# Another written-out order for the last attention chunk and the folds, with the folds' adds all on VectorE

## The chip, the cores and the metric

The kernel runs on one NeuronCore of a Trainium2 chip (trn2). The metric is device time in microseconds (us); a time of the kernel is the median over runs. The engines are called PE (TensorE), DVE (VectorE), ACT (ScalarE), POOL (GpSimd) and SP (SyncE, which issues the loads and stores). PEld is PE's weight load.

## The reference

The inputs are q, k, v (2 batches, 8 heads, 768 tokens, 64 features), a decay per head, and the weights of two MLPs (512 to 2048 to 512). The reference runs retention in blocks, then a 2-D Fourier transform's real part with an MLP, then a second MLP:

```python
for b in range(nb):                      # retention
    intra = einsum('bhic,bhjc->bhij', qb, kb) * Dmask
    intra = einsum('bhij,bhjd->bhid', intra, vb)
    inter = einsum('bhid,bhde->bhie', qb * lam_pow, kv_state)
    out[:, :, sl] = intra + inter
    kv_state = lam_block * kv_state + einsum('bhsd,bhse->bhde', kb * rev_pow, vb)
X = fft(fft(x, axis=1), axis=2)          # x: [2, 768, 512]
u = x + real(X)
u = u + relu(layernorm(u) @ w_ch1) @ w_ch2
return u + relu(layernorm(u) * g_ln @ w2_ch1) @ w2_ch2
```

## The kernel before

**Tiling.** The 768 tokens of a batch are six chunks of 128. Retention goes chunk by chunk. Chunks 3 to 5 are laid in mirrored order into the upper half of the tile U, so that the first transform (along the tokens) can fold token t with token 768 - t; row 0 of each mirrored tile has to be moved to its neighbour, which ACT does with copies of one row. Each fold gives an even half (cosine) and an odd half (sine), and each half is folded once more along the features. Five groups of matmuls for each of three folds then make the first transform, a second transform follows, then a layer norm and the first MLP. Values that must keep more than 16 bits are held as a high and a low float16 half; ACT makes the high half (a cast), POOL or DVE the low one (a subtraction). Weights arrive as 64-bit numbers in DRAM and are put together from bit fields: ACT takes the upper part (top), DVE shifts the lower part, DVE joins both (or), then come the two halves.

**What sets the order.** Up to the last chunk of the first batch, and again behind the layer norm of its first half, a planner lays the instructions out by simulated time and by priorities. Between these two, the order on PE, DVE, POOL and ACT is written out by hand in the string ORDER (line 44). Each word of it advances one chain by one step (line 957 on), and each engine works through its own instructions in that order. The words are:

- S: the score matmuls of chunk 5 (PE). B1, B0: the masked scores of the two heads' halves: DVE multiply with the mask (L353), ACT high half (L356), POOL low half (L358).
- s: the state behind chunk 4: POOL decay (L451), PE matmuls (L458), DVE add (L465), two ACT copies (L470).
- O4, O5: the outputs of chunks 4 and 5: 24 PE matmuls (L426), DVE sum into u (L432), ACT row copies. The matmuls need both halves of the masked scores.
- I: chunk 5's part from the state: PE matmuls (L375), DVE scaling into int (L379). O5's sum needs it.
- k0 to k2, j0 to j2: the cosine and the sine half of fold 0, 1, 2 (fold_half): an add or subtraction of two tiles in SBUF (L489), a half-fold (L491), two quarters (L494 and L495, or L497 and L498). The add runs on POOL if the fold's name, e0 to e2 for k and o0 to o2 for j, is in the string ONPOOL (line 50), otherwise on DVE.
- R: the fold of row 0 alone: four POOL instructions (L408 to L411), an ACT cast (L414), a POOL low half (L416).
- c0 to c3: the conversion of the first four weight chunks (conv_steps).
- d24, d20, ...: the first transform's matmuls of fold 2 for group 4, and so on. Those of fold 0 close a group; d04, d01 and d00 are followed by two matmuls with the row's halves. D0 to D4: ACT copies of the groups' results.
- q, X, p, P: the second transform, with a subtraction on DVE and, for X1 and X2, one on POOL. b, n: the layer norm; its power (L650) is on POOL. W: warm-up matmuls on PE whose results nobody reads, so many as the number says. M: the first MLP's first matmuls.

**Buffers near the change.** The score matmuls use two of three PSUM banks called "at"; d24 and d23 use that pool next. A weight chunk's joined value lies in one of three buffers (wtp), so c3 uses that of c0. The row fold and fold 0's odd half use the same place in SBUF, one after the other.

Of the kernel before, what the change touches and what calls it, by code (L numbers as in the profile page):

```python
# [20 lines left out]
B, H, S, D = 2, 8, 768, 64  # L21
# [20 lines left out]
YS = 2.0 ** -15  # L42

ORDER = """
c0 S B1 s O4 B0 O4 B0 O4 B1 s s c0 R k2 j2 s k2 c0 B0 I B1 c0 I k2 O5 O5 j2 c1 O5 j2 W12 d24 O5 d20 j1 k1 c3
k1 k0 k1 j1 d21 d22 k0 j1 d23 j0 j0 k0 j0 W6 d10 c2 d11 d14 R d13 d12 d03 c3 d02 D3 R c2 c1 c3 D2 d04 d01 D4
d00 D1 q0 D0 q0 c3 q2 q2 X0 X0 q1 q1 X1 p0 p1 P0 c1 X1 P1 b0 b1 b0 X2 c2 p2 b0 b1 X2 c1 P2 c2 b0 n0 b1 b2 b1
W27 n0 b2 n1 n0 b2 W6 n1 n0 b2 M00 n2 n1 n2 n2 n1 M01 M12 M11 M10 n2 M22 M20 M02 M21
"""
ONPOOL = "Y1 Y2 o0 o1 k0 k1 k2 j0 j1 j2"  # L50
LD1 = ()
LD2 = ()
EARLY0, GATEN, B1, SPC, DS, DC, DFO, DD, D1S, D2S, AO, YA, NR, NE, LN1, L1, L2, F01, F02, TL, R1, R2, SE, PR1, LAG, UB, FB, NW, MQ, SPL = 11, 8, 3, 2.0, 2.0, 5, 1.0, 0.5, 0.5, 1.0, "aba", "aa", 2, 0, 2, 2.5, 2.5, 16, 4, 3, 1.5, 2, "dddd_dppp", 0, 3, 3, 13, 11, 1, 3
# [71 lines left out]
def tile_retention_fourier_mlp(ctx: ExitStack, tc: tile.TileContext, a: dict, out: bass.AP):  # L125
# [20 lines left out]
    def bank(which, name):  # L146
        return banks[which].tile([P, 512], F32, tag=which, name=name)
# [103 lines left out]
    def w_load(kind, m, i, room=None):  # L251
        t = room
        if t is None:
            t = wst.tile([P, 512, 2], I32, tag="ws", name=f"ws{kind}_{m}_{i}")
        staged[kind, m, i] = t
        return sp.dma_start(t.rearrange("p n two -> p (n two)").bitcast(I16)[:, :2047], w_src(kind, m, i).bitcast(I16)[:, 1:2048])
# [11 lines left out]
    def w_conv(kind, m, i):  # L268
        return run(conv_steps(kind, m, i, "at"))
# [13 lines left out]
    def conv_steps(kind, m, i, which=None, into=None):  # L283
        if (kind, m, i) not in staged:
            w_load(kind, m, i)
        raw = staged.pop((kind, m, i))
        top = tops[n_top[0] % 3]
        n_top[0] += 1
        t = wtp.tile([P, 512], F32, tag="wt", name=f"wf{kind}_{m}_{i}")
        ti = t.bitcast(I32)  # L290
        part = ti if which is None else bank(which, f"ps_w{kind}_{m}_{i}").bitcast(I32)
        act.activation(top[:, :, 1], raw.bitcast(BF16)[:, :, 2], AF.Copy, scale=TOPS)  # L292
        dve.tensor_scalar(part, raw[:, :, 0], 13, None, op0=ALU.logical_shift_right)  # L293
        yield t
        dve.tensor_tensor(ti, part, top.rearrange("p n two -> p (n two)").bitcast(I32), op=ALU.bitwise_or)  # L295
        yield t
        if kind == 1:
            g, k = divmod(i, 4)
            if (m, g) not in w1t:
                w1t[m, g] = wpool.tile([P, 2, 4, 512], F16, tag=f"w1_{g}", name=f"w1_{m}_{g}")  # L300
            hi, lo = w1t[m, g][:, 0, k], w1t[m, g][:, 1, k]
        else:
            if into is None:
                into = w2t[m, i] = wpool.tile([P, 2, 512], F16, tag=f"w2_{i}", name=f"w2_{m}_{i}")
            hi, lo = into[:, 0], into[:, 1]
        if kind == 1 and m == 1:
            act.activation(t, t, AF.Copy, scale=gcol[:, k:k + 1])  # L307
        act.copy(hi, t)  # L308
        yield t
        (dve if m == 0 and i in (LD1 if kind == 1 else LD2) else pool).tensor_tensor(lo, t, hi, op=ALU.subtract)  # L310
        yield t
# [57 lines left out]
    def attn_i_steps(b, c, bk):  # L369
        t = f32t(f"int{b}_{c}")  # L370
        lp_ = lp[:, 1 if c >= 3 else 0]
        if b == 0:
            ps = bank(bk["i"], f"ps_i{b}_{c}")
            for i in range(H // 2):
                pe.matmul(ps[:, i * P:(i + 1) * P], loaded["qt", b, c][:, i * P:(i + 1) * P], diag[(c - 1) % 2][:, i],  # L375
                          start=True, stop=True)
            yield
            to, ti = (z.rearrange("p (h d) -> p h d", h=H) for z in (t, ps))
            dve.tensor_tensor(to, ti, lp_.unsqueeze(2).to_broadcast([P, H, D]), op=ALU.mult)  # L379
            xt[b, c] = t  # L380
            yield
            return
        both = [bank(bk["i"], f"ps_i{b}_{c}_{e}") for e in range(2)]
        with tc.manual_schedule(engines={mybir.EngineType.PE}):
            for i in range(H // 2):
                for e, ps in enumerate(both):
                    cols, r = slice(i * D, (i + 1) * D), slice(e * D, (e + 1) * D)
                    pe.matmul(ps[:, cols], loaded["qt", b, c][r, i * P:(i + 1) * P], states[(c - 1) % 2][r, cols],
                              start=True, stop=True)
        yield  # L390
        for e, ps in enumerate(both):
            to = t.rearrange("p (i e d) -> p i e d", e=2, d=D)[:, :, e]
            ti = ps[:, :H // 2 * D].rearrange("p (i d) -> p i d", d=D)
            dve.tensor_tensor(to, ti, lp_[:, e::2].unsqueeze(2).to_broadcast([P, H // 2, D]), op=ALU.mult)
        xt[b, c] = t
        yield
# [23 lines left out]
    def attn_o_steps(b, c, bk):  # L420
        ps = bank(bk["o"], f"ps_o{b}_{c}")
        for h in range(H):
            (i, e), hc = divmod(h, 2), slice(h * D, (h + 1) * D)
            m_, mc = ms[b, c, e], slice(i * P, (i + 1) * P)
            for n, (x, y) in enumerate(PASS):
                pe.matmul(ps[:, hc], m_[:, x, mc], vs[b, c][:, y, hc], start=n == 0, stop=n == 2)  # L426
        yield
        x_ = U[b][c] if c < 3 else U[b][8 - c]
        if c == 0:
            dve.tensor_scalar(x_, ps, XS, None, op0=ALU.mult)  # L430
        else:
            dve.scalar_tensor_tensor(x_, ps, XS, xt[b, c], op0=ALU.mult, op1=ALU.add)  # L432
        yield
        if c == 3:
            row0[b] = f32t(f"row0{b}", 4 if b == 0 else None)
            act.copy(row0[b][0:1], x_[0:1])
            if b > 0:
                run(row_fold(b))
        elif c > 3:
            act.copy(U[b][9 - c][0:1], x_[0:1])  # L440
        yield
        if c == NCH - 1:
            act.copy(x_[0:1], row0[b][0:1])
        yield

    def attn_s_steps(b, c, bk):
        new, old = states[c % 2], states[(c - 1) % 2]
        if c > 0:
            dec = stp.tile([P, H // 2 * D], F32, tag="dec", name=f"dec{b}_{c}")
            do, di = (z.rearrange("p (i d) -> p i d", d=D) for z in (dec, old))  # L450
            pool.tensor_tensor(do, di, lc.unsqueeze(2).to_broadcast([P, H // 2, D]), op=ALU.mult)  # L451
        yield
        k_ = ks[b, c]
        ps = bank(bk["st"], f"ps_st{b}_{c}")
        for h in range(H):
            (i, e), hc = divmod(h, 2), slice(h * D, (h + 1) * D)
            for n, (x, y) in enumerate(PASS):
                pe.matmul(ps[e * D:(e + 1) * D, i * D:(i + 1) * D], k_[:, x, hc], vs[b, c][:, y, hc],  # L458
                          start=n == 0, stop=n == 2)
        yield  # L460
        psv = ps[:, :H // 2 * D]
        if c == 0:
            dve.tensor_copy(new, psv)
        else:
            dve.tensor_tensor(new, psv, dec, op=ALU.add)  # L465
        yield
        if b == 0:
            for e in range(2):
                r = slice(e * D, (e + 1) * D)
                act.copy(diag[c % 2][r, :, e * D:(e + 1) * D], new[r].rearrange("p (i d) -> p i d", d=D))  # L470
        yield
# [456 lines left out]
    def eng(n):  # L928
        return pool if n in ONPOOL.split() else dve

    wide = {}
    chains = {"s": lambda: attn_s_steps(0, 4, bk0), "O4": lambda: attn_o_steps(0, 4, bk0),
              "O5": lambda: attn_o_steps(0, 5, bk0), "I": lambda: attn_i_steps(0, 5, bk0), "R": lambda: row_fold(0)}
# [5 lines left out]
    for g in range(5):  # L939
        chains[f"D{g}"] = lambda g=g: dft1_out(0, g, ps1[g])  # L940
    for i in range(NE, 4):
        chains[f"c{i}"] = lambda i=i: conv_steps(1, 0, i)
    for j in range(3):
        chains[f"q{j}"] = lambda j=j: dft2_q(0, j, bk0)
        chains[f"X{j}"] = lambda j=j: sub_sin(0, j, eng(f"Y{j}"))
# [59 lines left out]
    for c in range(NCH):  # L1005
        t = B1 + SPC * c
# [29 lines left out]
    n0 = (NB - 1) * NF  # L1036
# [16 lines left out]
    def step(n):  # L1053
        m = n // (NB * NF)
        return m, order[m][n // NF % NB], n % NF
# [3 lines left out]
    for (m, blk), f in fast_from.items():  # L1059
        for kk in range(2):  # L1060
            if m == 0 and blk < 3:
                put(16 * blk + f / 2 + kk - 3, lambda blk=blk, kk=kk: un_sums(0, blk, kk))
            else:
                at = m * NB * NF + order[m].index(blk) * NF
# [4 lines left out]
    for n in range(total + LAG):  # L1069
        rest = None  # L1070
        if n < total:
            m, blk, f = step(n)
# [34 lines left out]
```

## Time and profile before

| | |
|---|---|
| time, median of 3 runs | 611.54 us (611.45 to 612.33) |
| profiled execution | 611.77 us, its span 610.0 us |
| PE busy | 580.4 us, 95% of the span |
| DVE busy | 416.1 us, 68% |
| POOL busy | 285.9 us, 47% |
| ACT busy | 263.4 us, 43% |
| DMA | 63.23 MB, mean 104 GB/s |

The profile is of one execution. A busy share is an average over the whole span; the stages differ. The page also cuts the span into 40 slices of 15.25 us and gives the busy tenths of each engine; PE's begin with 6 8 6 9 9 and go on with 9 nearly everywhere. The written-out order covers about 32 to 75 us. The granted clock of PE is a share of full speed: 1.00 is the 2.4 GHz level, 0.50 the 1.2 GHz level.

### The profile page before, as it was taken

How to read it: one execution, taken by the hardware profiler on the slowest of the kernel's cores; microseconds unless marked ns; L12 is line 12 of the kernel's file. 1: busy time of each engine (PE TensorE's matmuls, PEld its weight loads, DVE VectorE, ACT ScalarE, POOL GpSimd, SP SyncE). 2: the span in 40 equal slices, each digit the busy share in tenths (PEclk: the TensorE clock that was granted, in tenths of full speed). 3: DMA queues.
4: the chain of work that ended last, by engine and by line, in shares of the span. 5: the costliest groups of instructions: out<-in, count | busy, mean ns of one | idle time of the engine just before them, and what ended most of it. 6: DMA issues, size and time to landing. Idle time of an engine off the chain costs nothing.

```text
span 610.0 us, 11891 instructions
## 1 busy us (share of the span) xinstructions
PE 580.4 (95%) x4675; PEld 381.4 (63%) x4675; DVE 416.1 (68%) x903; ACT 263.4 (43%) x530; POOL 285.9 (47%) x296
## 2 busy tenths in 40 slices
PE   6869989999999999899997999999999999999997
PEld 3754845566554555576765776666677677777773
DVE  5995699876596589886697778877444653445333
ACT  3644489764232433443456665853222222221120
POOL 7864879995443585451348765963021200020000
PEclk8878999999999999999998999999999999999999
DMA  8994149973000010353153542510111025102001
GB/s 278 396 401 135 44 133 268 337 243 122 2 1 0 19 35 2 81 144 121 45 163 119 177 158 99 162 33 1 53 27 27 2 74 66 18 1 81 24 1 52
DMA packets 46326, 63.23 MB, mean 104 GB/s; under 512 B 26176, under 2 KB 28350, under 8 KB 46270
## 3 DMA queue, kind: packets, MB, share of 16 engines
q1 hardware_dynamic: 45598, 62.40, 33.3%
q8 instruction: 36, 0.59, 0.4%
q10 hardware_dynamic: 672, 0.08, 0.1%
q14 instruction: 20, 0.16, 0.1%
HBM read 52.23 MB, written 6.29 MB: 96 GB/s over the span
## 4 chain that ended last, share of the span: by engine, by line
PE 59%; DVE 21%; ACT 8%; POOL 6%; issue 4%; DMA 1%; SPq 0%; DVEq 0%; ACTq 0%; POOLq 0%
PE ps_y L848 27%; PE ps L801 20%; PE ps_h L708 4%; DVE ps_w L293 3%; DVE wf L295 3%; PE ps_d L515 2%; DVE bst L642 2%; POOL m L358 2%; DVE tr L761 1%; ACT top L292 1%; PE ps_d L518 1%; ACT wf L307 1%; ACT w L308 1%; POOL w L310 1%; POOL kd L322 1%
## 5 line engine op out<-in xcount | busy, mean ns | idle before, releaser
L848 PE MATMUL ps_y<-w,h 128*128 128x512 f16 x1152 | 281.9, 380 | 3.5 <-ACT h L833 1.7
L848 PEld LDWEIGHTS <-h 128*128 128x128 f16 x1152 | 109.4, 98 | 102.5 <-ACT h L833 3.7
L801 PEld LDWEIGHTS <-sw 128*128 128x128 f16 x1104 | 95.2, 98 | 23.3 <-issue 7.1
L801 PE MATMUL ps<-th,sw 128*128 128x192 f16 x828 | 93.1, 247 | 5.1 <-DVE s L814 3.6
L310 POOL TENSOR_TENSOR w<-wf,w 128x512 f16<-128x512 f32 x58 | 67.2, 1165 | 38.7 <-ACT w L308 38.6
L801 PEld LDWEIGHTS <-w 128*128 128x128 f16 x828 | 72.3, 98 | 19.0 <-issue 0.8
L708 PE MATMUL ps_h<-unT,w 128*128 128x384 f16 x396 | 73.7, 326 | 1.7 <-DVE h L723 1.6
L833 ACT ACTIVATE h<-ps 128x384 f16<-128x384 f32 x92 | 43.7, 488 | 73.1 <-DVE ps L827 68.7
L801 PE MATMUL ps<-unT,w 128*128 128x192 f16 x552 | 63.4, 248 | 0.0
L834 DVE SCALAR_TENSOR_TENSOR h<-ps,h 128x384 f16<-128x384 f32 x92 | 49.6, 554 | 14.1 <-ACT h L833 12.6
L708 PEld LDWEIGHTS <-w 128*128 128x128 f16 x396 | 36.9, 98 | 29.8 <-issue 3.1
L753 POOL TENSOR_TENSOR sw<-ws,sw 128x512 f16<-128x512 f32 x32 | 37.9, 1199 | 33.9 <-ACT sw L752 33.8
L292 ACT ACTIVATE top<-ws 128x512 f16<-128x512 bf16 x57 | 44.4, 778 | 16.3 <-DVE wf L295 15.9
L821 DVE TENSOR_TENSOR t<-ps,s 128x192 f32<-128x192 f32 x46 | 16.3, 354 | 49.7 <-PE ps L801 49.5
L813 ACT COPY s<-ps 128x192 f32<-128x192 f32 x46 | 14.5, 315 | 73.0 <-PE ps L801 73.0
L671 POOL TENSOR_TENSOR uns<-un,uns 128x512 f16<-128x512 f32 x21 | 24.6, 1172 | 43.8 <-ACT uns L670 43.7
L777 POOL TENSOR_TENSOR th<-ts,th 128x384 f16<-128x384 f32 x24 | 22.2, 942 | 42.9 <-ACT th L776 42.9
L295 DVE TENSOR_TENSOR wf<-ps_w,top 128x512 int32<-128x512 int32 x60 | 40.6, 682 | 2.4 <-POOL w L310 1.2
L308 ACT CAST w<-wf 128x512 f16<-128x512 f32 x58 | 34.9, 608 | 10.3 <-DVE wf L295 10.1
L293 DVE TENSOR_SCALAR ps_w<-ws 128x512 int32<-128x512 int32 x54 | 37.1, 689 | 0.9
L827 DVE TENSOR_TENSOR ps<-ps,s 128x192 f32<-128x192 f32 x46 | 16.7, 362 | 28.6 <-PE ps L801 28.4
L814 DVE TENSOR_TENSOR s<-ps,s 128x192 f32<-128x192 f32 x46 | 16.2, 353 | 28.2 <-ACT s L813 28.1
(162 smaller groups left out, 822.0 us busy)
## 6 DMA issues: line engine op xcount, KB each, us to landing
ws<-in_w SPq DMA_DIRECT2D x25, 511.8 KB, 3.9
ws<-in_w2b SPq DMA_DIRECT2D x16, 511.8 KB, 3.5
ws<-in_w1b SPq DMA_DIRECT2D x16, 511.8 KB, 3.7
kt<-in_kt SPq DMA_DIRECT2D x12, 256.0 KB, 4.1
qt<-in_qt SPq DMA_DIRECT2D x12, 256.0 KB, 5.7
v<-in_v SPq DMA_DIRECT2D x12, 256.0 KB
k<-in_k SPq DMA_DIRECT2D x12, 256.0 KB, 6.2
pre<-in_w SPq DMA_DIRECT2D x4, 511.8 KB
```

Source lines behind the costliest of these rows:

```text
L292: act.activation(top[:, :, 1], raw.bitcast(BF16)[:, :, 2], AF.Copy, scale=TOPS)
L293: dve.tensor_scalar(part, raw[:, :, 0], 13, None, op0=ALU.logical_shift_right)
L295: dve.tensor_tensor(ti, part, top.rearrange("p n two -> p (n two)").bitcast(I32), op=ALU.bitwise_or)
L308: act.copy(hi, t)
L310: (dve if m == 0 and i in (LD1 if kind == 1 else LD2) else pool).tensor_tensor(lo, t, hi, op=ALU.subtract)
L671: pool.tensor_tensor(s_[:, 1], un, s_[:, 0], op=ALU.subtract)
L708: pe.matmul(ps, w[:, i, k, fo:fo + P], x[:, j, k, :], start=n == 0, stop=n == 11)
L753: pool.tensor_tensor(lo, z, hi, op=ALU.subtract)
L801: pe.matmul(ps, lhs, rhs, start=start and n == 0, stop=n == 5, skip_group_check=True)
L833: act.activation(hi, z, AF.Relu)
L834: dve.scalar_tensor_tensor(lo, z, 0.0, hi, op0=ALU.max, op1=ALU.subtract)
L848: pe.matmul(dn[blk][j], h[:, x, j * P:(j + 1) * P], w[:, y], start=f == 0 and n == 0, stop=f == NF - 1 and n == 2)
```

## The change

ORDER is written anew from its start to the second transform. In the new order the two masked scores (B1, B0) come first, the state's matmuls stand ahead of O4, the conversion c0 goes on only behind the sum of O4, the row fold starts behind the masked scores' low halves, O5 and its row copies come ahead of all folds, and the folds run one after the other: k2 and j2, k1, j1, j0, k0. The second cast of the row (R) moves behind the copy D3. The conversions of c1 to c3 follow the folds on DVE, their ACT and POOL steps lie between those of the second transform. Six warm-up matmuls (W6) ahead of d10 fall away, and the groups of fold 1 come in another order. ONPOOL loses the names that put o0 and o1 on POOL; its names k0 to k2 and j0 to j2 are asked for nowhere. In conv_steps the shift on DVE moves from the first step to the second, so the first step is ACT's alone; and c0's shift writes to a PSUM bank of "at" and not in place. Everything behind n0 is unchanged.

```diff
--- before.py
+++ after.py
@@ -42,12 +42,12 @@
 YS = 2.0 ** -15
 
 ORDER = """
-c0 S B1 s O4 B0 O4 B0 O4 B1 s s c0 R k2 j2 s k2 c0 B0 I B1 c0 I k2 O5 O5 j2 c1 O5 j2 W12 d24 O5 d20 j1 k1 c3
-k1 k0 k1 j1 d21 d22 k0 j1 d23 j0 j0 k0 j0 W6 d10 c2 d11 d14 R d13 d12 d03 c3 d02 D3 R c2 c1 c3 D2 d04 d01 D4
-d00 D1 q0 D0 q0 c3 q2 q2 X0 X0 q1 q1 X1 p0 p1 P0 c1 X1 P1 b0 b1 b0 X2 c2 p2 b0 b1 X2 c1 P2 c2 b0 n0 b1 b2 b1
+c0 S B1 B0 s s B1 B0 s s O4 B1 B0 O4 c0 I O4 R I O5 O5 O5 O5 c0 c1 c2 W12 k2 j2 k2 k2 d24 d20 d21 j2 j2 d22 d23
+k1 k1 k1 d14 d10 d11 j1 j1 j1 d12 d13 c3 j0 j0 j0 d03 k0 k0 k0 d02 c1 D3 R c2 R c0 D2 d04 d01 D4 d00 c3 D1 q0 D0 q0
+c1 q2 q2 X0 X0 q1 q1 c2 X1 p0 p1 P0 c1 X1 P1 b0 b1 b0 X2 c3 p2 c2 b0 b1 X2 P2 c3 b0 n0 b1 b2 b1
 W27 n0 b2 n1 n0 b2 W6 n1 n0 b2 M00 n2 n1 n2 n2 n1 M01 M12 M11 M10 n2 M22 M20 M02 M21
 """
-ONPOOL = "Y1 Y2 o0 o1 k0 k1 k2 j0 j1 j2"
+ONPOOL = "Y1 Y2"
 LD1 = ()
 LD2 = ()
 EARLY0, GATEN, B1, SPC, DS, DC, DFO, DD, D1S, D2S, AO, YA, NR, NE, LN1, L1, L2, F01, F02, TL, R1, R2, SE, PR1, LAG, UB, FB, NW, MQ, SPL = 11, 8, 3, 2.0, 2.0, 5, 1.0, 0.5, 0.5, 1.0, "aba", "aa", 2, 0, 2, 2.5, 2.5, 16, 4, 3, 1.5, 2, "dddd_dppp", 0, 3, 3, 13, 11, 1, 3
@@ -290,8 +290,8 @@
         ti = t.bitcast(I32)
         part = ti if which is None else bank(which, f"ps_w{kind}_{m}_{i}").bitcast(I32)
         act.activation(top[:, :, 1], raw.bitcast(BF16)[:, :, 2], AF.Copy, scale=TOPS)
+        yield t
         dve.tensor_scalar(part, raw[:, :, 0], 13, None, op0=ALU.logical_shift_right)
-        yield t
         dve.tensor_tensor(ti, part, top.rearrange("p n two -> p (n two)").bitcast(I32), op=ALU.bitwise_or)
         yield t
         if kind == 1:
@@ -939,7 +939,7 @@
     for g in range(5):
         chains[f"D{g}"] = lambda g=g: dft1_out(0, g, ps1[g])
     for i in range(NE, 4):
-        chains[f"c{i}"] = lambda i=i: conv_steps(1, 0, i)
+        chains[f"c{i}"] = lambda i=i: conv_steps(1, 0, i, None if i else "at")
     for j in range(3):
         chains[f"q{j}"] = lambda j=j: dft2_q(0, j, bk0)
         chains[f"X{j}"] = lambda j=j: sub_sin(0, j, eng(f"Y{j}"))
```

## Rows read from the trace of the kernel before

**Rows 1.** Windows: length, busy of PE, PEld, DVE, ACT, POOL, clock, DMA.

```profile
75.00:130.00 55.00, 53.20 (x432) 30.40 (x431) 50.52 (x88) 44.23 (x82) 50.90 (x48) 1.00 0.80 246
240.00:610.00 370.00, 356.78 (x2831) 247.98 (x2829) 229.10 (x540) 141.83 (x290) 121.65 (x127) 0.99 0.26 71
```

**Rows 2.** Chain of waits, 15 to 82 us: start, length, what.

```profile
26.03 0.83 DVE wf L293
...
37.41 4.61 DVE e L489
...
43.61 2.72 PE warm L964 x12
46.33 5.03 PE ps_d L515 x10
51.36 0.66 PE warm L964 x6
52.01 5.55 PE ps_d L515 x16
...
60.52 1.53 PE ps_pq L577 x12
```

**Rows 3.** Timeline of DVE, 25 to 54 us: start, length, instruction, idle before.

```profile
26.78 0.68 DVE L432 SCALAR_TENSOR_TENSOR u<-ps_o,int 128x512 f32<-128x512 f32 x1
...
33.36 1.27 DVE L353 SCALAR_TENSOR_TENSOR m<-ps_s,mask 128x512 f32<-128x512 f32 x2
...
37.32 4.70 DVE L489 TENSOR_TENSOR e<-u 128x512 f32<-128x512 f32 x1
...
46.48 0.42 DVE L491 TENSOR_TENSOR e<-e 128x255 f32<-128x255 f32 x1
46.82 0.69 DVE L489 TENSOR_TENSOR e<-u 128x512 f32<-128x512 f32 x1
47.42 0.29 DVE L494 TENSOR_TENSOR f<-e 128x128 f32<-128x128 f32 x1
47.62 0.29 DVE L495 TENSOR_TENSOR f<-e 128x129 f32<-128x129 f32 x1
49.06 1.47 DVE L491 TENSOR_TENSOR o<-o 128x255 f32<-128x255 f32 x1 [1.15 <-POOL o L489]
```

**Rows 4.** Timeline of POOL, 30 to 68 us.

```profile
31.13 3.83 POOL L358 TENSOR_TENSOR m<-m,m 128x512 f16<-128x512 f32 x3
35.95 0.71 POOL L408 TENSOR_TENSOR rc<-row 1x255 f32<-1x255 f32 x1 [0.99 <-ACT row L436]
...
38.09 2.26 POOL L358 TENSOR_TENSOR m<-m,m 128x512 f16<-128x512 f32 x2
40.32 1.14 POOL L310 TENSOR_TENSOR w<-wf,w 128x512 f16<-128x512 f32 x1
45.34 4.91 POOL L489 TENSOR_TENSOR o<-u 128x512 f32<-128x512 f32 x2 [3.88 <-ACT u L440]
50.21 0.85 POOL L416 TENSOR_TENSOR rhl<-r,rhl 1x257 f16<-1x257 f32 x1
...
64.23 2.27 POOL L310 TENSOR_TENSOR w<-wf,w 128x512 f16<-128x512 f32 x2
66.92 0.56 POOL L650 TENSOR_TENSOR rs<-rs,neghalf 128x1 f32<-128x1 f32 x1 [0.42 <-DVE mv L645]
```

**Rows 5.** Timeline of PE, 22 to 62 us.

```profile
35.02 0.73 PE L426 MATMUL ps_o<-vhl,m 128*128 128x64 f16 x19 [0.85 <-POOL m L358]
...
38.47 1.45 PE L375 MATMUL ps_i<-diag,qt 128*128 128x128 f32 x8 [2.22 <-ACT diag L470]
```

**Rows 6.** Windows as in rows 1, around the clock's fall and rise.

```profile
36.00:39.00 3.00, 0.78 (x20) 0.67 (x15) 3.00 (x4) 2.40 (x6) 2.92 (x5) 1.00 1.04 414
39.00:49.00 10.00, 7.78 (x46) 4.59 (x45) 8.91 (x17) 3.53 (x7) 6.12 (x5) 0.51 0.96 353
50.00:61.00 11.00, 11.00 (x42) 4.80 (x40) 5.03 (x13) 4.84 (x9) 2.21 (x3) 1.00 0.33 103
```

## The prediction

> **What bounds the kernel now.** I read the page first: PE is busy 95% of the span, but in 40 slices its digits fall to 6 in the first and third, so the weak stretch lies ahead of the first MLP, which is where the order of the diff applies. The windows come next. From 240 us on PE is busy 356.78 of 370 us, so what happens late is matmul work and any start that comes earlier should be passed on; from 75 to 130 us VectorE (50.52 of 55), GpSimd (50.90) and PE (53.20) are all nearly full, and none of them waits there for a fixed moment [rows 1]. Then the chain of waits between 26 and 61 us, which names the path: a shift of a weight chunk on DVE at 26.03, one fold add that takes 4.61 us, 2.72 us of warm-up matmuls behind it, then the transform's matmuls until the second transform starts at 60.52 [rows 2]. Last come the timelines of DVE, GpSimd and PE in that stretch, for durations and for who stood in whose way [rows 3 to 5].
>
> The reader should see two things there. First, the add of k2 (L489, two operands in SBUF) is recorded with 4.70 us from 37.32, while the same instruction on a later fold takes 0.69 [rows 3]. Over that time GpSimd runs, without a gap, the end of the row fold, the two low halves of the masked scores (2.26) and a weight's low half (1.14, to 41.46); the add ends 0.56 after that, one plain add [rows 4]. So an add with two SBUF operands waited until GpSimd's queue had a gap, over several instructions. Behind it in DVE's queue stood int, which the warm-up matmuls wait for, and u of O5. Second, the reverse: the adds of o1 and o0 on GpSimd are recorded with 4.91 for two [rows 4], over a time when DVE runs adds back to back; DVE then has to wait 1.15 us for o1 [rows 3].
>
> **The change part by part.** The sum is made against the profiled execution: span 610.0, time 611.77, so 1.77 lie around the span. The median of the three runs is 611.54, 0.23 less; I take the difference in time from the median. Consecutive DVE instructions overlap by a little, so I price them by the distance of starts: an add 46.82 to 47.42 = 0.60, a half-fold 46.48 to 46.82 = 0.34, a quarter 47.42 to 47.62 = 0.20 [rows 3]. One half (k or j) is 0.60 + 0.34 + 2 x 0.20 = 1.34.
>
> Step 1, c0's shift. It leaves its place at 26.03, ahead of u of chunk 2, which starts at 26.78: 0.75 of the path [rows 2, 3]. It now goes into a PSUM bank behind u of O4, where DVE waits for the I matmuls anyway. I take -0.7. Bounds: 0, if GpSimd's low halves hold the path there, and -0.8.
>
> Step 2, the way to the first transform matmul d24. In the times of before: the masked scores leave DVE at 33.36 + 1.27 = 34.63 [rows 3]; GpSimd is free of chunk 4's low halves at 31.13 + 3.83 = 34.96 [rows 4]. Now the two low halves of chunk 5 come directly behind: 34.96 + 2.26 = 37.2. The state matmuls go ahead of O4, into the time in which O4 waits for those halves of chunk 4, so the state's copies are done when O4 ends at 35.02 + 0.73 = 35.75 [rows 5]. Allow 0.4 for the copies: I runs 36.2 to 37.5 (its row says 1.45, part of it at the lower clock), O5 (24 matmuls at 0.73/19) to 38.4, int on DVE to 38.1, u of O5 to 39.1. The row fold's four GpSimd instructions take 2.14 (35.95 to 38.09) [rows 4], now from 37.2 to 39.35. The k2 add waits for them at most 0.3, then 0.60 + 0.60 (j2's add) + 0.34 + 0.40 give 41.3, and d24 at 41.4 instead of 46.33 [rows 2]: -4.9. The warm-up matmuls end before that even at 2.72. Row copies lie on ACT behind u of O5, and k1 needs them only at 42.0. Bounds: -3.9 (the row fold and its neighbours each hold DVE up for their own length, 1.0 in all) and -5.3 (no hold-up, I at 1.1).
>
> Step 3, the transform's matmuls. Eight of them in a row take 5.55, 0.69 each; the first five took 5.03 [rows 2], since the granted clock was 0.51 of full between 39 and 49 us (the 1.2 GHz level for most of it), after 3 us with only 0.78 us of PE work; between 50 and 61 it was 1.00 [rows 6]. In the new order I, O5 and the warm-up follow O4 closely, so I expect the full clock: 5.03 - 3.45 = -1.6. W6 falls away, -0.66 [rows 2]. VectorE feeds them in time: by 0.69 each, PE comes to d03 10 x 0.69 = 6.9 after d24, while j2's rest and k1, j1, j0 take 0.74 + 3 x 1.34 = 4.8. The two adds that come over from GpSimd cost 1.2 of DVE beside PE's work; if that cover were gone they would cost that. One new wait: the row's low half now goes to GpSimd behind ACT's copy of D3. From the end of d03 that is one copy, one cast and 0.85 [rows 4], together some 1.9, while PE has d02 and d04, 1.4: +0.5. Bounds 0 and +1.5. Sum of the step -1.76.
>
> Step 4, the tail to the layer norm. Three weights' low halves instead of two stand on GpSimd between the second transform and the layer norm's first power; two take 2.27 and end 0.42 before that power starts [rows 4]. One more of 1.13 overruns by 0.7; and DVE's X2 subtraction has two SBUF operands and can meet it. I take +0.8, bounds 0 and +1.2. A wait is added on DVE too: the shift of c3 needs the buffer of c0, so GpSimd's low half of c0, now behind the row's. Behind it stand or3 and X0 alone, and X0 needs the second transform anyway: nothing, or +0.5 if the row's half is late. SP's load that refills c1's buffer waits for c1's shift, which now stands behind all folds: it goes out a little later, for a weight that is read in the stretch after 75 us.
>
> Sum: -0.7 - 4.9 - 1.76 + 0.8 = **-6.56 us**. I pass all of it on through the stretches of [rows 1]: 611.54 - 6.56 = 605.0. The bounds, step by step: least 0 - 3.9 + (0 - 0.66 + 1.5) + 1.2 = -1.9, so 609.6; most -0.8 - 5.3 - (1.6 + 0.66) + 0 = -8.4, so 603.1.
>
> One rule speaks against the folds on VectorE. The Trainium skill, "SBUF — State Buffer", Who interferes with whom, says that a VectorE instruction with two SBUF inputs and a GpSimd instruction that reads SBUF exclude each other, and that the one issued first has the shared pair for its whole instruction. By the rule, for one instruction at a time, the k2 add would have waited for about 1.1 us; the row shows 4.1 of waiting. What it would make of the new order is the second rival.
>
> **The rivals.**
> (1) The clock is at its lower level again when d24 starts. For it: PE still idles between the warm-up and d24, about 1.5. Against it: before the fall PE had done 0.78 us of work between 36 and 39 [rows 6]; in the new order I, O5 and most of the warm-up fall into that time. Price 1.6: 606.6.
> (2) The folds shut GpSimd out. DVE now runs six halves back to back, 8 us with two SBUF operands. If it starts them before the row fold is through, the row fold stands until DVE pauses, as o1 did [rows 4]. The pause comes when j0's add needs the buffer that the row fold releases: 2.1 of GpSimd work, of which about 1.0 reaches PE. 606.0. Against it: the row fold can start 1.9 before the k2 add.
> (3) The gain is given back between 75 and 130 us, where three engines are full and work was laid out behind the old start; the weights are fetched there, and the transfers' share is 0.80 [rows 1]. If they rather than DVE set the pace, perhaps two thirds are lost: 609.4. Against it: their buffers come free by DVE's shifts, so they move with them.
> (4) Slower: the instructions behind the written-out block are placed by a planner from simulated times, and these change. PE idles 370 - 356.78 = 13.2 us after 240 [rows 1]. If another layout added more than 6.6 to that, half as much again, the kernel would be slower; two thirds more (8.8) gives 613.8. Against it: the tasks and their due steps are the same.
> That the change doesn't do what it says is hardly open: the order is fixed on four engines, and of the names taken from the list only o0 and o1 were ever asked for, so only two adds move.
>
> **How the numbers follow.** Forecast 605.0, chance 0.56, own range 603.7 to 606.3; rival 1 0.14, rival 2 0.06, rival 3 0.13 (0.05 of it so near to before that it can't be told), rival 4 0.07; 0.04 for more than the bounds' sum, about 602. The range 602.5 to 609.8 takes in both bounds' sums and leaves out rival 4, the last case and the worse half of rival 3. A measurement of this kernel can tell about 0.2%, 1.2 us. Faster 0.88, the same 0.05, slower 0.07.
>
> **What would show it.** Right: no fold add on GpSimd and none over 1.1 on DVE; d24 near 40.7; a granted clock of 1.00 from there; the second transform near 53.2 instead of 60.52; the layer norm's first power about 6.5 earlier than 66.92, and the same distance at 130 and at the end. Step 1 is wrong if chunk 3's masked scores start no earlier; step 3 if the clock is 0.5 at d24, or if PE stands longer than 0.5 at the row's matmul. The whole is wrong if the layer norm comes 6 us earlier and the last store doesn't: then rival 3 or 4 holds, and the windows from 75 on show which engine lost it.

## The result, and the profile after

| | before | changed |
|---|---|---|
| median, same chip | 612.07 us (611.45 to 613.45, 6 runs) | 606.47 us (605.02 to 609.08, 6 runs) |
| profiled execution, its span | 611.77, 610.0 | 605.77, 603.9 |

The ratio is 0.9908, interval 0.9882 to 0.9934: 5.6 us less (4.0 to 7.2), where 6.56 were forecast. Between the two profiled executions the difference is 6.0. So the kernel is faster, within the range on record, and some 1 us short of the forecast's size. Single executions of one kernel lie up to some 4 us apart.

The windows of the changed kernel answer [rows 1, 6]; the columns are the same. The last window ends with the span.

```profile
36.00:39.00 3.00, 2.52 (x39) 2.35 (x40) 2.82 (x6) 0.96 (x2) 2.62 (x5) 1.00 1.02 400
39.00:49.00 10.00, 8.61 (x31) 4.28 (x29) 9.55 (x27) 3.69 (x7) 0.00 (x0) 1.00 0.80 302
...
75.00:130.00 55.00, 53.74 (x418) 30.54 (x416) 49.06 (x83) 44.09 (x82) 52.23 (x50) 1.00 0.83 250
240.00:603.90 363.90, 352.31 (x2808) 245.69 (x2806) 224.85 (x530) 139.06 (x285) 117.11 (x123) 0.99 0.28 73
```

Between 36 and 39 us PE now works 2.52 of 3 us instead of 0.78, and from 39 to 49 the granted clock is 1.00 instead of 0.51. GpSimd, 6.12 busy there before, does nothing in those ten microseconds.

DVE's timeline answers [rows 3] (start, length, instruction, idle before):

```profile
26.52 0.68 DVE L432 SCALAR_TENSOR_TENSOR u<-ps_o,int 128x512 f32<-128x512 f32 x1
...
38.38 0.69 DVE L432 SCALAR_TENSOR_TENSOR u<-ps_o,int 128x512 f32<-128x512 f32 x1
38.99 0.68 DVE L489 TENSOR_TENSOR e<-u 128x512 f32<-128x512 f32 x1
...
41.92 0.69 DVE L489 TENSOR_TENSOR e<-u 128x512 f32<-128x512 f32 x1
...
43.52 0.68 DVE L489 TENSOR_TENSOR o<-u 128x512 f32<-128x512 f32 x1
...
49.94 2.24 DVE L295 TENSOR_TENSOR wf<-wf,top 128x512 int32<-128x512 int32 x1
```

The reader should see k2's add at 38.99 with 0.68 instead of 4.70, directly behind u of O5, and the distance from one half of a fold to the next, 43.52 - 41.92 = 1.60. GpSimd's timeline answers [rows 4]:

```profile
30.87 6.07 POOL L358 TENSOR_TENSOR m<-m,m 128x512 f16<-128x512 f32 x5
...
38.25 0.45 POOL L411 TENSOR_TENSOR r<-rc 1x129 f32<-1x129 f32 x1
49.85 0.67 POOL L416 TENSOR_TENSOR rhl<-r,rhl 1x257 f16<-1x257 f32 x1 [11.15 <-DVE wf L294]
...
59.25 1.14 POOL L310 TENSOR_TENSOR w<-wf,w 128x512 f16<-128x512 f32 x1
60.82 0.56 POOL L650 TENSOR_TENSOR rs<-rs,neghalf 128x1 f32<-128x1 f32 x1 [0.43 <-DVE rs L648]
```

The row fold is done at 38.70, before the first fold add: there neither engine is held up. The last DVE row above shows the old pattern at a new place. The or at 49.94 takes 2.24 instead of 0.69 beside two GpSimd instructions without a gap (the last ends at 51.63), and it ends 0.55 after them. PE's timeline answers [rows 5] and the transform's rows of the chain in [rows 2]:

```profile
36.40 1.16 PE L375 MATMUL ps_i<-diag,qt 128*128 128x128 f32 x8 [0.90 <-ACT diag L470]
...
41.20 2.30 PE L515 MATMUL ps_d<-cs,f 128*1 128x385 f32 x6 [1.39 <-DVE f L495]
...
50.27 0.62 PE L523 MATMUL ps_d<-cr,rhl 1*1 1x385 f16 x2
...
53.36 1.60 PE L577 MATMUL ps_pq<-cdsd,cst 128*128 128x128 f32 x12
```

To compare in one view, these are d24 and q0 in PE's timeline of the kernel before (it has them 0.07 ahead of the chain of [rows 2]):

```profile
46.26 3.81 PE L515 MATMUL ps_d<-cs,f 128*1 128x385 f32 x6
...
60.45 1.60 PE L577 MATMUL ps_pq<-cdsd,cst 128*128 128x128 f32 x12
```

So d24 starts 5.06 earlier, q0 7.09, and the layer norm's first power 66.92 - 60.82 = 6.10. A group of matmuls near 130 us, 128.27 before, starts at 122.17, again 6.10 earlier, and from the power to the end of the span it is 543.08 in both kernels: all of it arrives. The chain of waits in the changed kernel shows where the path went:

```profile
47.41 0.44 DVE e L491
...
49.94 2.25 DVE wf L295
...
53.35 0.79 ACT top L292
...
59.50 1.18 DVE u L585
```

The first transform's matmuls, 5.03 and 5.55 in [rows 2], are not on it any more. It runs through DVE's folds, a weight's or, ACT's queue, and the X2 subtraction (L585), though PE is still busy without a pause from 41.20 to q0: the two now end close together.

### The profile page after: what moved, and what is told of

The parts are those of the page before. It is cut to its first block, busy times and chain, and to the rows that moved or that the text cites. A ratio compares the mean times of both kernels' runs of the same rounds, so it can differ in the third digit from the quotient of the medians.

```text
span 603.9 us, 11882 instructions
## 1 busy us (share of the span) xinstructions
PE 576.7 (95%) x4669; PEld 379.3 (63%) x4669; DVE 416.1 (69%) x905; ACT 262.8 (44%) x530; POOL 280.0 (46%) x294
## 4 chain that ended last, share of the span: by engine, by line
PE 62%; DVE 19%; ACT 7%; POOL 6%; issue 4%; DMA 1%; SPq 0%; DVEq 0%; POOLq 0%; ACTq 0%
PE ps_y L848 30%; PE ps L801 22%; PE ps_h L708 4%; DVE wf L295 2%; DVE bst L642 2%; ACT top L292 2%; DVE ps_w L294 2%; DVE tr L761 2%; PE ps_d L518 1%; POOL m L358 1%; POOL w L310 1%; PE ps_s L346 1%; PE ps_i L388 1%; POOL kd L322 1%; ACT w L308 1%
## 5 line engine op out<-in xcount | busy, mean ns | idle before, releaser
L310 POOL TENSOR_TENSOR w<-wf,w 128x512 f16<-128x512 f32 x58 | 67.1, 1164 | 36.3 <-ACT w L308 36.2
L671 POOL TENSOR_TENSOR uns<-un,uns 128x512 f16<-128x512 f32 x21 | 24.6, 1171 | 43.6 <-ACT uns L670 43.4
```

The costliest lines, as they stand in the source:

```text
L671: pool.tensor_tensor(s_[:, 1], un, s_[:, 0], op=ALU.subtract)
```

## The experiments

All times are medians beside the kernel before on the same chip. The changed kernel was run again in three of the four comparisons, without an edit, to have it on the same chip as what it is held against.

> The changed kernel once more, for its spread: its six times lie between 605.0 and 609.1, those of before between 611.5 and 613.5. Theory A: a slower execution is one in which PE's granted clock is at 0.5 for longer (the mean clocks of the six are 0.980 for 609.08 and 0.992 for 605.02); then the profile of an execution near 608 shows a stretch at 0.5 that the first profile hasn't, most likely at the first transform's first matmuls, behind about 1.4 us in which PE waits for k2's fold (price 1.6 us). Theory B: it is the race for SBUF between VectorE and GpSimd ahead of 30 us; then the second transform starts about 1 us later at the same clocks. Expected median 605 to 607.5, ratio to before 0.989 to 0.993.

605.42 us against 612.35, ratio 0.9887 (0.9869 to 0.9906).

> The changed kernel, to stand beside the run with the shorter tail on the same chip: ratio to before 0.987 to 0.992, and from the layer norm's first power to the end 543.1 as in the two profiles of it so far and in that of before (543.1), whatever the time at which the power starts.

606.16 against 612.41, ratio 0.9918 (0.9890 to 0.9946).

> The changed kernel once more, beside the last one on the same chip. 605 to 606.5. Its profile also says which of two orders was taken near 20.7 us: with VectorE's low half of v ahead of GpSimd's decay, u of chunk 2 starts 0.75 earlier than a kernel with the shift ahead of it (step 1 as priced); with GpSimd ahead, only 0.2 to 0.3 earlier.

606.14 against 612.66, ratio 0.9901 (0.9885 to 0.9917). With the first comparison's 0.9908 the mean of the four ratios is 0.9904; "the changed kernel" below is that share of the same chip's before where it was not run itself.

**Was the long add the length of GpSimd's queue?** The kernel before, with the low half of c0 taken out of GpSimd's run:

```diff
-... k2 j2 s k2 c0 B0 I B1 c0 I k2 O5 ... d23 j0 j0 k0 ...
+... k2 j2 s k2 c0 B0 I B1 I k2 O5 ... d23 j0 c0 j0 k0 ...
```

> The kernel before with one step moved: the GpSimd low half of c0 (1.14 us) goes from behind the masked scores' low halves to behind j0's add, so GpSimd's unbroken stretch ends at about 40.3 instead of 41.46. Theory A (an add with two SBUF operands waits until GpSimd's queue has a gap, however many instructions that takes): k2's add is 1.1 shorter, near 3.6, and ends near 40.9; the first transform starts 1.1 earlier, and the time falls by 1.0 to 1.1, to 610.9 or so. Rival (the add loses only to one instruction at a time, and something else held it): the add stays at 4.7 and the time at 612.0.

610.90 us against 612.35, ratio 0.9982 (0.9964 to 1.0000): the size that was expected, at the edge of what can be told. Its executions lie from 609.2 to 614.0, and the profiled one (609.37) is one of the short ones. DVE's timeline, then GpSimd's:

```profile
37.23 3.59 DVE L489 TENSOR_TENSOR e<-u 128x512 f32<-128x512 f32 x1
```

```profile
38.01 2.26 POOL L358 TENSOR_TENSOR m<-m,m 128x512 f16<-128x512 f32 x2
44.16 3.69 POOL L489 TENSOR_TENSOR o<-u 128x512 f32<-128x512 f32 x1 [3.88 <-ACT u L440]
```

The add is 4.70 - 3.59 = 1.11 shorter, by one low half (1.14 in [rows 4]), and ends 0.55 after GpSimd's run does, 37.23 + 3.59 against 38.01 + 2.26. It did wait for the whole run. In that profile d24 starts 1.20 earlier than before, and its first six matmuls take 2.72 instead of 3.81; the granted clock from 39 to 49 us is 0.66 there and 0.51 before. The second row shows the other direction: o1's add on GpSimd takes 3.69 while DVE works through adds.

**Order alone, adds alone.** The changed kernel with o0 and o1 on GpSimd again; then the kernel before with them on DVE:

```diff
-ONPOOL = "Y1 Y2"
+ONPOOL = "Y1 Y2 o0 o1"
```

> The changed kernel with o0 and o1 on GpSimd again, all else as changed. Theory A (the order is what counts, the adds' engine little): GpSimd's adds have to wait for a gap in VectorE's folds and VectorE then for them; each costs VectorE 1.26 instead of 0.70 plus a wait, together 1.5 to 3 on its way to the last fold at 48.4, of which PE's slack there (the matmuls of fold 0 start 1.2 later than the fold's end) hides 1.2: 0.3 to 1.8 slower than the changed kernel, 606.5 to 608. Rival (the move of the adds carries a good part of the gain): 3 us slower or more, 609.5.

610.77 us against 612.35, ratio 0.9974 (0.9958 to 0.9989): 5.35 more than the changed kernel on the same chip, outside 606.5 to 608 and on the rival's side. DVE's, GpSimd's and PE's timelines:

```profile
40.57 1.50 DVE L491 TENSOR_TENSOR e<-e 128x255 f32<-128x255 f32 x1
42.11 1.25 DVE L494 TENSOR_TENSOR f<-e 128x128 f32<-128x128 f32 x1
```

```profile
40.24 2.97 POOL L489 TENSOR_TENSOR o<-u 128x512 f32<-128x512 f32 x2 [1.16 <-ACT u L440]
```

```profile
43.62 3.69 PE L515 MATMUL ps_d<-cs,f 128*1 128x385 f32 x6 [3.43 <-DVE f L495]
```

The two GpSimd adds get in between k2's steps. Its half-fold and its first quarter, each of which needs the result of the instruction before, take 1.50 and 1.25 instead of 0.42 and 0.29. From the start of its add, k2's fold takes 4.19 instead of 2.16. PE idles 3.43 instead of 1.39, the clock falls (0.60 from 43.6 to 47.3), and the first six matmuls take 3.69 instead of 2.30. Between this profiled execution and the first one of the changed kernel the whole difference is 3.9; what makes up the rest of the 5.35 isn't shown.

```diff
-ONPOOL = "Y1 Y2 o0 o1 k0 k1 k2 j0 j1 j2"
+ONPOOL = "Y1 Y2"
```

> The kernel before with o0 and o1 on VectorE and nothing else changed: the counterpart of the run that put them back on GpSimd in the changed kernel, where 4 to 5 us were lost. Theory A (the adds matter only in the new order, since in the old one PE's transform matmuls run without a gap from 46.3 to 60.5 and never wait for a fold): the wait of 1.15 us for o1 disappears on VectorE, the last fold ends some 2 us earlier, and the time stays within 0.5 of before, 611.8 to 612.8. Rival (the adds carry the gain by themselves): 608 or less.

611.99 us against 612.88, ratio 0.9991 (0.9978 to 1.0003): nothing that can be told. The long add stays. DVE's timeline:

```profile
38.69 0.68 DVE L489 TENSOR_TENSOR e<-u 128x512 f32<-128x512 f32 x1
39.30 4.70 DVE L489 TENSOR_TENSOR o<-u 128x512 f32<-128x512 f32 x1
```

GpSimd's run came later in that execution (the clock was at 0.66 over 26 to 36 us), so k2's add got through and j2's took the same 4.70. By the ratios, everything but the adds gives 1.6 us (0.7 to 2.6), the adds alone 0.6 (-0.2 to 1.3), and both together 5.9: more than twice the sum of the two.

**The shift of c0 (step 1).** The changed kernel with that shift first and in place:

```diff
-        yield t
+        if not (kind == 1 and m == 0 and i == 0):
+            yield t
         dve.tensor_scalar(part, raw[:, :, 0], 13, None, op0=ALU.logical_shift_right)
+        if kind == 1 and m == 0 and i == 0:
+            yield t
...
-        chains[f"c{i}"] = lambda i=i: conv_steps(1, 0, i, None if i else "at")
+        chains[f"c{i}"] = lambda i=i: conv_steps(1, 0, i)
```

> The changed kernel with c0's shift where it was: in the first step and in place, ahead of chunk 2's sum. By the prediction's step 1 it costs 0.7 of the path: the changed kernel's 605.4 to 606.5 becomes 606.1 to 607.2, and in the profile chunk 2's sum starts 0.75 behind the end of the value's low half (vhl). Rival (the low halves on GpSimd or the variation ahead of 26 us hide it): no difference.

608.04 us against 612.88, ratio 0.993 (0.991 to 0.995); the changed kernel's 0.9904 would be 607.0, so 1.0 more by the medians and 1.6 by the ratios (0.4 to 2.8 by this interval alone). In the profile u of chunk 2 starts at 26.71, 0.75 behind the shift's start, as in [rows 3]. But the clock also fell there, to 0.66 over 26 to 36 us, so its d24 at 43.00 isn't the shift's price alone.

What the changed kernel's own profiles say is clearer. In the first one u of chunk 2 starts only 0.26 earlier than before, in the second (e9_again, 605.05 us) 0.75 earlier. First DVE and GpSimd of the first, then of the second:

```profile
20.80 1.07 DVE L327 SCALAR_TENSOR_TENSOR vhl<-v,vhl 128x512 f16<-128x512 f32 x1
21.80 1.64 DVE L332 TENSOR_TENSOR khl<-kd,khl 128x512 f16<-128x512 f32 x1
```

```profile
20.71 0.62 POOL L451 TENSOR_TENSOR dec<-state,lc 128x256 f32<-128x256 f32 x1
```

```profile
20.74 0.68 DVE L327 SCALAR_TENSOR_TENSOR vhl<-v,vhl 128x512 f16<-128x512 f32 x1
21.33 1.10 DVE L332 TENSOR_TENSOR khl<-kd,khl 128x512 f16<-128x512 f32 x1
...
26.03 0.68 DVE L432 SCALAR_TENSOR_TENSOR u<-ps_o,int 128x512 f32<-128x512 f32 x1
```

```profile
20.78 1.10 POOL L451 TENSOR_TENSOR dec<-state,lc 128x256 f32<-128x256 f32 x1
```

Ahead of anything that the change touches, a low half on DVE and the state's decay on GpSimd start within 0.1 us of each other. With GpSimd first, DVE's two low halves end at 23.44, with DVE first at 22.43: 1.0 of DVE's time turns on who is 0.04 to 0.09 ahead. The later wait for ACT's vhl takes in half of it. Of the fourteen profiles (before, changed and the twelve runs) only the first of the changed kernel has GpSimd first there.

The same happens 5 us earlier, between another low half on DVE and a product on GpSimd. In e9_again DVE is first, at 15.54 against 15.58, and its low half takes 0.69. In e0_again's profile, of an execution of 606.26 us, GpSimd is first:

```profile
15.69 1.51 DVE L327 SCALAR_TENSOR_TENSOR vhl<-v,vhl 128x512 f16<-128x512 f32 x1 [0.51 <-ACT vhl L326]
```

```profile
15.61 2.49 POOL L322 TENSOR_TENSOR kd<-k,rev 128x512 f32<-128x512 f32 x2
```

There u of chunk 2 starts at 26.95 and the second transform at 53.80, both 0.92 later than in e9_again, at a clock of 1.00 in both from 20 us on to the tail. GpSimd is first at this place in four of the fourteen profiles (e0_again, e1_warm28, e3_o_on_pool, e8_tail), and in these four the granted clock from 10 to 13 us is 0.50, against 0.64 to 0.85 in the others. That these trades are chance is read from the profiles, not forced by an edit.

**The clock ahead of d24 (rival 1).** More warm-up matmuls, then fewer, in the changed kernel:

```diff
-... c0 c1 c2 W12 k2 j2 k2 k2 d24 ...
+... c0 c1 c2 W28 k2 j2 k2 k2 d24 ...
```

> The changed kernel with 28 warm-up matmuls ahead of the first transform in place of 12, so that PE no longer waits 1.4 us for k2's fold (16 more at 0.12 each are 1.9 us; they end about 0.4 after that fold). Theory A (the spread is the clock falling in that wait): the clock stays at 1.00 from 26 to 75 us in every execution, the highest time falls below 607, and the median is 605 to 605.8. Theory B (the spread comes from elsewhere): the spread stays at about 4 us, and the median goes up by the 0.3 to 0.5 that the surplus matmuls cost.

607.19 us against 612.35, ratio 0.992 (0.9897 to 0.9944), 1.8 more than the changed kernel there, and the spread stays (605.65 to 609.58). The profiled execution is one of its longer ones, 609.37. Its windows, then PE:

```profile
26.00:36.00 10.00, 7.82 (x79) 6.87 (x76) 8.56 (x13) 4.44 (x9) 7.27 (x7) 0.71 1.03 402
39.00:49.00 10.00, 9.92 (x74) 6.26 (x74) 9.58 (x25) 3.87 (x7) 1.72 (x5) 1.00 0.79 295
58.00:64.00 6.00, 6.00 (x31) 4.40 (x31) 5.57 (x14) 1.90 (x7) 5.30 (x6) 0.74 0.21 78
```

```profile
30.70 2.06 PE L375 MATMUL ps_i<-diag,qt 128*128 128x128 f32 x8
32.69 2.07 PE L346 MATMUL ps_s<-qt,kt 64*128 64x128 f32 x14
```

The clock is 1.00 around d24 here too, and low in two other places: ahead of the new block, where chunk 4's part from the state and chunk 5's scores take 2.06 and 2.07 (in the first profile of the changed kernel the scores take 1.16), and again in the tail. PE had waited 1.22 for a low half ahead of the first; the same wait of 1.22 stands in the first profile of the changed kernel, where no fall follows, so the wait alone doesn't explain it. So the spread doesn't come from a fall at d24. What the profiles offer for the changed kernel's 604.9 to 609.2 are falls like these and the trade of places near 15.6 us. Which of them its executions above 606.3 meet isn't shown, as none of those was profiled; the longest execution of the first comparison has a mean clock of 0.980, the shortest 0.992. The kernel before spreads as widely on its own, 610.5 to 614.0.

```diff
-... c0 c1 c2 W12 k2 j2 k2 k2 d24 ...
+... c0 c1 c2 W2 k2 j2 k2 k2 d24 ...
```

> The changed kernel with 2 warm-up matmuls ahead of the first transform in place of 12, so that PE stands for about 2.5 us before d24 instead of 1.4. Theory A (the granted clock falls when PE has had little work for a while): the clock is at 0.5 for the first matmuls of the transform in most executions, and the time is 1.4 to 2 us above the changed kernel, 607 to 608.5. Rival (the work of O4, I and O5 is enough, the warm-up does nothing there): the same as the changed kernel within 0.3.

609.88 us against 612.88, ratio 0.997 (0.9945 to 0.9995), 2.9 more than the changed kernel by the medians and 4.0 by the ratios. The executions lie from 607.6 to 615.6, and the profiled one is the shortest. PE's timeline:

```profile
37.81 0.38 PE L964 MATMUL warm<-expo 128*128 128x256 f16 x2
40.67 2.97 PE L515 MATMUL ps_d<-cs,f 128*1 128x385 f32 x6 [2.49 <-DVE f L495]
43.44 2.52 PE L515 MATMUL ps_d<-sn,f 128*128 128x384 f32 x4
```

PE was idle for 2.49 instead of 1.39, and the clock falls just behind d24 (0.68 from 43 to 47 us; 2.97 and 2.52 instead of 2.30 and 1.45). In all four profiles with the twelve matmuls it is 1.00 there.

**Is every microsecond passed on (rivals 3 and 4)?** The changed kernel with twenty warm-up matmuls ahead of the second transform:

```diff
-... c3 D1 q0 D0 q0
+... c3 D1 W20 q0 D0 q0
```

> The changed kernel with 20 warm-up matmuls put ahead of the second transform, a delay of known size on the path: 20 at 0.115 are 2.3 us. Theory A (everything behind is moved as a whole): the layer norm's first power and the last instruction are both 2.3 later, and the time is 2.3 above the changed kernel's, near 608. Rival (the three full engines between 75 and 130 us have slack that takes part of a shift, so that a gain ahead of them is lost in part too): less than 1.2 at the end.

608.99 us against 612.88, ratio 0.9948 (0.9928 to 0.9967), 2.0 more than the changed kernel by the medians and 2.7 by the ratios. In the profile q0 starts 54.96 - 52.77 = 2.19 later than PE was ready for it. The stretch from the first power to the end of the span, from the profiles:

| kernel | first power | span | rest |
|---|---|---|---|
| before | 66.92 | 610.0 | 543.08 |
| changed | 60.82 | 603.9 | 543.08 |
| changed, e9_again | 60.33 | 603.3 | 542.97 |
| e2_before_c0_late | 64.65 | 607.6 | 542.95 |
| e3_o_on_pool | 64.75 | 607.9 | 543.15 |
| e7_delay | 62.07 | 606.0 | 543.93 |

In all fourteen profiles, with the power anywhere from 59.3 to 67.4, the rest is 542.95 to 543.93. A gain ahead of the power is not given back behind it.

**The tail from q0 to the first power.** It grew from 6.47 to 7.46. Two attempts on the changed kernel. The first takes c1's halves ahead of the second transform and c2's low half behind X1:

```diff
-... D4 d00 c3 D1 q0 D0 q0
-c1 q2 q2 X0 X0 q1 q1 c2 X1 p0 p1 P0 c1 X1 P1 b0 b1 b0 X2 c3 p2 c2 b0 b1 X2 P2 c3 b0 ...
+... D4 c1 c1 d00 c3 D1 q0 D0 q0
+q2 q2 X0 X0 q1 q1 c2 X1 p0 p1 P0 X1 P1 b0 b1 b0 c2 X2 c3 p2 b0 b1 X2 P2 c3 b0 ...
```

> The changed kernel with the last two steps of c1 (ACT's high half, GpSimd's low half) ahead of the second transform instead of inside it, and c2's low half behind X1: two low halves instead of three then stand on GpSimd between the second transform and the layer norm's first power. Theory A (the tail is set by GpSimd's queue there, as step 4 of the prediction has it, 1.0 in the profile): the power starts about 0.9 earlier against the second transform's start, 6.5 instead of 7.46 behind it, and the time is 0.5 to 1.0 below the changed kernel measured beside it. Rival (the tail is set by ACT's copies and PE): the distance stays 7.4 and the time is the same.

606.06 us against 612.41, ratio 0.990 (0.9881 to 0.9919): the same as the changed kernel. DVE's and PE's timelines:

```profile
52.48 1.38 DVE L294 TENSOR_SCALAR wf<-pre 128x512 int32<-128x512 int32 x1
...
60.56 0.50 DVE L585 TENSOR_TENSOR u<-u,qs 128x257 f32<-128x257 f32 x1
```

```profile
56.20 0.49 PE L553 MATMUL ps_pq<-cdsd,cst 128*128 128x129 f32 x2 [0.85 <-ACT qs L580]
```

X2 takes 0.50 instead of 1.25, but the low half put earlier holds a weight's shift on DVE (1.38 instead of 0.41), the or behind it comes late, ACT's next top stands ahead of the last result copy, and PE waits 0.85. The distance stays 7.46: the conflict moved. The second attempt only puts c3's low half behind the third power:

```diff
-... X2 c3 p2 c2 b0 b1 X2 P2 c3 b0 n0 b1 b2 b1
-W27 n0 b2 n1 n0 b2 W6 n1 n0 b2 M00 ...
+... X2 c3 p2 c2 b0 b1 X2 P2 b0 n0 b1 b2 b1
+W27 n0 b2 n1 n0 b2 W6 n1 n0 b2 c3 M00 ...
```

> In the changed kernel the last of the three low halves in the tail (c3's) holds back X2's subtraction on VectorE, 1.25 us instead of 0.50, and the first layer norm's value for the power stands behind it in VectorE's queue. Here c3's low half goes to GpSimd behind the third power, everything else as in the changed kernel. Theory A (the tail's 1.0 us is mostly this one block): X2 takes 0.50, the first power comes 6.7 us after q0 instead of 7.46, and the time is 0.7 us less than the changed kernel's, if the first MLP's matmuls don't wait for the half (at most 0.3). Theory B (something else, the copies on ACT or X1's own wait, sets the power): the distance stays within 0.2 of 7.46 and the time is the same. Theory C: the half is too late for the first MLP, PE waits for it by 1 us or more and the time is no less.

605.90 us against 612.66, ratio 0.9898 (0.9879 to 0.9918); the changed kernel on that chip has 606.14, executions of both spread over 3 us, and 0.24 can't be told. The profile can be read. DVE, first X2 of the changed kernel, then two lines of this one; then its GpSimd:

```profile
59.43 1.25 DVE L585 TENSOR_TENSOR u<-u,qs 128x257 f32<-128x257 f32 x1
```

```profile
58.73 0.39 DVE L585 TENSOR_TENSOR u<-u,qs 128x257 f32<-128x257 f32 x1
...
62.93 0.63 DVE L661 SCALAR_TENSOR_TENSOR rs<-mv,rs 128x1 f32<-128x1 f32 x1
```

```profile
59.25 0.56 POOL L650 TENSOR_TENSOR rs<-rs,neghalf 128x1 f32<-128x1 f32 x1 [0.67 <-DVE rs L648]
...
62.82 0.73 POOL L605 TENSOR_TENSOR u<-u,qs 128x257 f32<-128x257 f32 x1
```

X2 is 0.86 shorter, and from q0 (52.66) to the power it is 6.59: 0.87 of the tail's 0.99 was this one block. About half is given back at the third layer norm, where a tiny DVE instruction with two SBUF operands takes 0.63 instead of 0.21, while a GpSimd subtraction runs: PE's 96 matmuls of the first MLP start at 64.95, 0.49 earlier than in the changed kernel's profile from the same chip, e11_again (65.44; 0.05 of it from q0), and the span is 602.7 against 603.3.

## Why the prediction was right, step by step

| | forecast | first profile | e9_again |
|---|---|---|---|
| d24 starts (before: 46.26) | 40.7 | 41.20 | 40.71 |
| d24 to q0 (before: 14.19) | -1.76 | -2.03 | -2.02 |
| q0 to the first power (before: 6.47) | +0.8 | +0.99 | +0.98 |
| first power to the end (before: 543.08) | 0 | 0.00 | -0.11 |

**Step 1** was priced right for the order of the engines that before's profile shows: 0.75 in e9_again, 0.7 forecast. In the first profile it gave 0.26, because the two instructions near 20.7 us had changed places. The step's lower bound of 0 named GpSimd's low halves as what could hold the path, not this. That e9_again's d24 meets the forecast to 0.01 is in part luck: it depends on such trades.

**Step 2** has the mechanism that the forecast gave: the long add waited for GpSimd's whole run (e2_before_c0_late), and once the run lies ahead of the folds it takes 0.68. Without step 1's part d24 comes 4.80 earlier in both profiles (5.06 - 0.26 and 5.55 - 0.75), where 4.9 were forecast. Inside the step two errors offset each other. The forecast's 36.2 for I is in the times of before; the first profile's 36.40 is 36.66 in these. It waits 0.90 for ACT's diag copies, which stand behind a row copy of chunk 3, and 0.4 was allowed. In return k2's add starts 2.59 after I, where the forecast had 2.9 and up to 0.3 of waiting for the row fold. No run moves the state's matmuls or the masked scores alone, so how the 4.80 divides between these moves and the add isn't shown; e2_before_c0_late has the price of one instruction of the run.

The Trainium skill, "SBUF — State Buffer", Who interferes with whom, says that a VectorE instruction with two SBUF inputs and a GpSimd instruction that reads SBUF exclude each other, and that the first has the ports for its whole instruction. The exclusion is seen here: k2's add takes 4.70 beside GpSimd's run and 0.68 with none. But the wait is not for one instruction: 4.70, and 3.59 with one instruction fewer in the run.

**Step 3** has nearly the right sum, -2.03 against -1.76, with terms that were off. The clock stayed up: by the starts, the first ten matmuls take 3.52 (41.20 to 44.72) instead of 4.93 (46.26 to 51.19), which is 1.4 less where 1.6 was forecast. W6's 0.66 falls away. The wait for the row's low half was put at 0.5 and is about 0.13: the first pair of the row's matmuls takes 0.62 at 50.27, the next two pairs 0.50 and 0.49, and PE shows no idle time. One half of a fold costs DVE 1.60 and not 1.34, since its half-fold and its quarters now stand right behind the instruction whose result they need, where [rows 3] has others in between. For the six halves that makes 9.29 (38.99 to 48.28) instead of 8.04, 1.25 more on DVE, which PE's work covers: the folds end at 48.4, and d04 starts at 49.53.

One sentence of the step fails: "The two adds that come over from GpSimd cost 1.2 of DVE beside PE's work; if that cover were gone they would cost that" is right as far as it goes, but it prices the move as a cost and gives it no gain. In the new order the same adds on GpSimd come in between k2's steps, and the kernel takes 5.35 more (e3_o_on_pool): without the move most of the gain is gone. I had read o1 and o0 as held up by DVE [rows 4]; between dependent DVE instructions they are the ones that hold DVE up.

**Step 4** is right in size, +0.8 against +0.99, and in the mechanism that it named second: X2's two SBUF operands meet the third low half. With that low half away, 0.87 of it goes (e10_c3_late). The first one it named, an overrun of GpSimd itself, didn't occur: the low half ends at 60.39, and the power starts at 60.82 behind DVE.

**Rival 1** didn't occur in any profile of the changed kernel: the clock is 1.00 at d24. It is the right kind of event in other places: e1_warm28 shows it at 31 to 36 us and in the tail. By before's profiled time the sum gave 611.77 - 6.56 = 605.2; the profiles of 605.77 and 605.05 are within 0.6 of that, so most of the 1.3 up to the median of 606.47 lies in longer executions. The longest execution with a profile, e0_again at 606.26, is 0.9 behind e9_again already at 20 us. For those above it the mean clocks suggest a fall somewhere, but which do, and why, stays open. **Rival 2** needed the folds to start before the row fold was through; it ended at 38.70 and the first add began at 38.99, a margin of 0.3, the same in all four profiles of the changed kernel. **Rivals 3 and 4** fall by the table of the first power and the span.

## What to carry to other kernels

If a VectorE instruction with two SBUF operands is recorded many times longer than its twin, add up what GpSimd runs without a gap beside it. Here the add lasted until the run was over, and one instruction of 1.14 taken out of the run made it 1.11 shorter. Move the whole run, not one end of it, and look where it lands next, as the tail's low halves show. A reorder and a change of engine that do little alone can be worth most of it together (1.6 and 0.6 against 5.9 here), so try the pair before discarding either.

## What was not expected of the hardware

- In these rows the engine that was in stayed in while its next instruction was ready. GpSimd's run kept k2's ready add waiting, 4.70 instead of 0.68. VectorE's ready adds did the same to GpSimd's add, 3.69 (e2_before_c0_late), and to its row half, 3.17 instead of 0.67 (e4_before_o_dve). Between dependent VectorE instructions GpSimd got in twice, and VectorE's half-fold took 1.50 instead of 0.42 (e3_o_on_pool).
- A start 0.04 to 0.09 us earlier on one of the two engines decided over 1.0 us of VectorE's time (the two profiles of the changed kernel near 20.7 us), and over 0.8 near 15.6 us (e0_again).
- A tiny instruction was held up too: one on 128x1 elements took 0.63 instead of 0.21 beside a GpSimd subtraction (e10_c3_late).
- Four VectorE instructions of one half of a fold, one behind the other, take 1.60 by their starts; by the distances of [rows 3], with independent ones between them, 1.34.
